# Key features by cyclic shifts in three products, dense queries spread through DRAM, and a third pair of banks, in a two-block attention kernel

## The chip, the cores and the metric

The kernel runs on one core of a Trainium2 chip. The metric is the device time of one execution in microseconds (us). Several executions are timed for each kernel, and one more is recorded by the profiler; its length is called the span, and is about 2 us shorter than the time (429.1 us for 431.45 in before). A run is called slow when it lies over 1.5% above the fastest of the same kernel; such runs are left out of every ratio.

Engines are named as the profile names them: PE (matmul), PEld (its weight loads), DVE (VectorE), ACT (ScalarE), POOL (GpSimd), SP (the queue that issues all DMAs here but two loads of 800 KB, which ACT issues). The sums of PE's matmuls land in the PSUM tile `ps`, which this kernel declares as eight banks of 512 fp32 numbers per partition, 0 to 7.

## The reference

Two attention blocks over different inputs, S = 2048, D = 640, 32 heads of 20, their outputs put side by side:

```python
def _A_ref(x, wqkv, wo):                       # softmax attention
    qkv = (x @ wqkv).reshape(B, S, 3, H, Dh).transpose(2, 0, 3, 1, 4)
    q, k, v = qkv[0], qkv[1], qkv[2]
    p = softmax(einsum("bhqd,bhkd->bhqk", q, k) * Dh ** -0.5)
    o = einsum("bhqk,bhkd->bhqd", p, v)
    return o.transpose(0, 2, 1, 3).reshape(B, S, D) @ wo

def _B_ref(x, wqkv, wo):                       # linear attention
    ...                                        # the same q, k, v
    phi = lambda t: where(t > 0, t + 1, exp(t)) + 1e-6
    pq, pk = phi(q), phi(k)
    num = einsum("bhqd,bhde->bhqe", pq, einsum("bhsd,bhse->bhde", pk, v))
    den = einsum("bhqd,bhd->bhq", pq, einsum("bhsd->bhd", pk))[..., None] + 1e-6
    return (num / den).transpose(0, 2, 1, 3).reshape(B, S, D) @ wo

output = concatenate([A, B], axis=-1)          # [1, 2048, 1280]
```

## The kernel before

Block A does not form the 2048 x 2048 scores. The scores are small, so the exponential is replaced by a polynomial of second order, and `exp(q.k)` becomes a scalar product of features: a constant, the 20 entries of k, and the 210 products of pairs of them. A guard on the chip checks that the scores are small and falls back to an exact path otherwise. So there are three stages:

1. For each of 16 tiles of 128 keys: project K and V, make the pair products on DVE and ACT (the tile `F`), and add `V^T F` into four banks on PE.
2. For each of 32 units (512 queries, 4 heads): a *select* matmul (`f_Qr`, `f_S`) puts sums of two query entries in banks, ACT squares them (four squares of 1024 columns per unit), a last group of matmuls multiplies the squares with the sums of stage 1, and DVE moves the result to `OTr`. After two units the *normaliser* follows: the denominators go out to DRAM, and come back as one 512 KB load `Rbc` that repeats them over partitions; a DVE multiply divides.
3. A rest, in which the last normalisers and the output projections run.

Block B has few dependences on A, and its matmuls fill gaps. The order of each engine's instructions is fixed when the kernel is built: a planner simulates the engines with durations written into the source, and takes the ready task with the lowest `prio` number. A wrong duration cannot give a wrong result, but it gives a poor order.

The parts (cuts marked with `...`):

```python
    NPS = 2          # buffers for the squares
    NP = 3           # buffers for pairs waiting for their normaliser
    NRB = 1          # buffers for the broadcast load

    def t_feat(self, t, deps):                 # 19 products a tile, of 64 to 640 elements
        ...
        sets = ((5, 10, 15), (1, 4, 9, 14, 19), (2, 7, 8, 13, 18), (3, 6, 11, 12, 16, 17))
        for ds in sets:
            def fn(_, ds=ds):
                for d in ds:
                    L = _DL[d]
                    o = self.F[:, s, :, _DO[d]:_DO[d] + L]
                    a = self.F[:, s, :, 220:220 + L]
                    b = self.Ks[:, s2, :, d - 1:d - 1 + L] if d % 2 else self.F[:, s, :, 220 + d:220 + d + L]
                    sch.op("dve", lambda e, o=o, a=a, b=b: e.tensor_tensor(o, a, b, op=ALU.mult), ...)
        ...

    def t_q(self, n, deps):                    # queries of one unit, weights padded from 20 to 32 columns
        ...
            for c in range(N_DC):
                self.fm(ps[:, b, :], self.wq[:, c, g, :], self.xT[:, qc, c, :], ...)

    def t_sel(self, n, k, deps):
        ...
            for i in range(4):
                sch.mm(ps[0:_NF, i, :], self.S2[...], self.Qr[32 * i:32 * i + 32, s, :], ...)   # banks 0 to 3
        j = self.plan.add(_Task("pe", 0.22, fn, prio=0.7, acq=("sA", "sB"), mode="sc"), deps)
        for p in range(2):                     # one square for banks 0, 1 and one for banks 2, 3
            ...

    def t_norm(self, P, evs):
        ...
        nb = nd.rearrange("(i u) q -> i (u q)", u=2).unsqueeze(1).broadcast_to([4, 32, 1024])
        d3 = self.spd([lambda e: e.dma_start(self.Rbc[:, rb].rearrange("p u q -> p (u q)"), nb)], (d2, prev), ...)

        def mult(_):
            sch.op("dve", lambda e: e.tensor_tensor(self.OTw[:, ow], self.OTr[:, pr], self.Rbc[:, rb], op=ALU.mult), ...)
        ...
```

## Time and profile before

| | before |
|---|---|
| time, median of the first 3 runs | 428.57 us (427.08 to 433.26) |
| busy: PE, DVE, ACT | 328.6, 304.1, 220.5 us of a span of 429.1 (the profiled run took 431.45 us) |
| span up to the first square | 177.7 us |
| first square to the end of the last | 198.0 us |
| after the last square | 53.4 us |

The three stretches are cut from the trace at the first and the last square of ACT. The busy tenths of the page, 40 slices of the span, show the stages: DVE full up to slice 16, PE full afterwards, a thin last eighth. PEclk is the clock that PE was granted, in tenths of full speed.

```profile
PE   3295677778777776899898778979998898765176
DVE  4849999999999999677678435546785686454631
ACT  1163457446354434587888676546766387600001
PEclk9998899999899989799999878789999898959589
```

The windows view gives busy times per stretch. Its columns are the stretch, its length, then the busy us and the number of instructions of PE, PEld, DVE, ACT and POOL, the granted clock, the DMA share and GB/s. The rows are the middle of stage 1, the squares, and the rest.

```profile
40.00:160.00 120.00, 91.40 (x2540) 64.43 (x2536) 112.04 (x320) 59.91 (x155) 0.00 (x0) 0.96 0.11 26
177.70:375.70 198.00, 173.31 (x2956) 81.47 (x2952) 128.29 (x251) 138.97 (x166) 0.00 (x0) 0.93 0.41 122
375.70:429.10 53.40, 30.18 (x541) 17.58 (x541) 22.44 (x47) 2.55 (x7) 0.00 (x0) 0.75 0.40 122
```

In stage 1 DVE is busy 112 of 120 us, and PE 91. In the squares PE is the fullest with 173 of 198. In the rest no engine is.

The costliest groups, from the page. After the bar stand busy us and the mean ns of one; after the second bar the idle time just before them and what ended it.

```profile
L1364 ACT ACTIVATE f_big<-ps 110x1024 bf16<-110x1024 f32 x128 | 123.8, 1026 | 50.5 <-PE ps L172 50.5
L1235 DVE TENSOR_TENSOR f_big<-f_big,f_Ks 128x512 bf16<-128x512 bf16 (+9 forms) x160 | 54.6, 345 | 4.4
L172 PE MATMUL ps<-f_xT,f_wq 128*32 128x512 bf16 x640 | 43.5, 413 | 1.0 <-DVE f_big L1393 1.0
L1235 DVE TENSOR_TENSOR f_big<-f_big 128x320 bf16<-128x320 bf16 (+3 forms) x144 | 47.6, 330 | 4.6
L1448 DVE TENSOR_TENSOR f_OTw<-f_big,f_Rbc 128x1024 bf16<-128x1024 f32 x15 | 18.3, 1221 | 20.7 <-DMA f_Rbc<-f_Nd 20.7
```

The two product groups are 102 us of DVE in 304 instructions. ACT waits 50.5 us for the selects. DVE waits 20.7 us for the broadcast load; DVE is not the bound of the squares.

The chain that ended last, by engine and by line:

```profile
PE 38%; DVE 37%; ACT 9%; DMA 8%; issue 3%; POOL 2%; SPq 1%; DVEq 0%; POOLq 0%; ACTq 0%
```

### The profile page before, as it was taken

The page shows a single profiled execution, that of the slowest core. Times are in us where ns is not written, and L with a number is a line of the kernel's source. Part 1 is how long each engine was busy: PE and PEld are TensorE (multiplying, and loading weights), DVE is VectorE, ACT ScalarE, POOL GpSimd, SP SyncE. Part 2 cuts the span into 40 slices and gives each one's busy share as a digit, 9 for nine tenths or more (in the row PEclk, how much of TensorE's full clock was granted, in tenths as well). Part 3 has the DMA queues.
Part 4 walks back from the last instruction along what each step waited for, and adds up shares of the span by engine and source line. Part 5 has one row for each costly group of instructions (what it writes and reads, how often), then busy time and mean ns, then how long its engine had stood idle before and what let it go on. Part 6 is the DMA issues. An engine that isn't in the chain of part 4 may idle for free.

```text
span 429.1 us, 14778 instructions
## 1 busy us (share of the span) xinstructions
PE 328.6 (77%) x6596; PEld 184.5 (43%) x6596; DVE 304.1 (71%) x734; ACT 220.5 (51%) x371; POOL 12.8 (3%) x52
## 2 busy tenths in 40 slices
PE   3295677778777776899898778979998898765176
PEld 0263454556455554565343222435344442443042
DVE  4849999999999999677678435546785686454631
ACT  1163457446354434587888676546766387600001
POOL 6400000000000000000000000000000000000000
PEclk9998899999899989799999878789999898959589
DMA  8969530000000000000413455733345644684131
GB/s 290 255 147 122 112 128 2 4 3 3 3 4 3 2 4 3 2 4 5 130 55 108 136 131 173 223 133 113 115 131 155 192 127 118 191 229 155 57 110 65
DMA packets 53124, 42.26 MB, mean 98 GB/s; under 512 B 22624, under 2 KB 48576, under 8 KB 53056
## 3 DMA queue, kind: packets, MB, share of 16 engines
q1 hardware_dynamic: 51744, 39.64, 33.3%
q10 hardware_dynamic: 1312, 1.64, 1.0%
q8 instruction: 52, 0.85, 0.8%
q14 instruction: 16, 0.13, 0.1%
HBM read 23.63 MB, written 13.19 MB: 86 GB/s over the span
## 4 chain that ended last, share of the span: by engine, by line
PE 38%; DVE 37%; ACT 9%; DMA 8%; issue 3%; POOL 2%; SPq 1%; DVEq 0%; POOLq 0%; ACTq 0%
PE ps L172 38%; DVE f_big L1235 23%; ACT f_big L1364 8%; DMA out_dram<-f_st 5%; DVE f_kn L1241 2%; DVE f_pk L1529 2%; DVE f_r L1521 2%; DMA f_Rbc<-f_Nd 2%; POOL f_it L1114 1%; SPq L1666 1%; DVE f_st L1026 1%; DVE f_CT L1138 1%; DMA f_w<-f_Od 1%; ACT f_ex L1525 1%; DVE f_big L1393 1%
## 5 line engine op out<-in xcount | busy, mean ns | idle before, releaser
L1364 ACT ACTIVATE f_big<-ps 110x1024 bf16<-110x1024 f32 x128 | 123.8, 1026 | 50.5 <-PE ps L172 50.5
L172 PE MATMUL ps<-f_w,f_xT 128*32 128x320 bf16 x1280 | 52.4, 319 | 13.3 <-ACT f_ex L1525 9.4
L1235 DVE TENSOR_TENSOR f_big<-f_big,f_Ks 128x512 bf16<-128x512 bf16 (+9 forms) x160 | 54.6, 345 | 4.4
L172 PE MATMUL ps<-f_wB,f_xB 128*32 128x320 bf16 x1280 | 51.6, 310 | 4.7 <-DVE f_woB L1599 2.5
L1235 DVE TENSOR_TENSOR f_big<-f_big 128x320 bf16<-128x320 bf16 (+3 forms) x144 | 47.6, 330 | 4.6
L1525 ACT ACTIVATE f_ex<-ps 128x320 f32<-128x320 f32 (+1 forms) x52 | 26.0, 500 | 44.0 <-DVE f_r L1521 43.8
L172 PEld LDWEIGHTS ps<-f_w,f_xT 128*32 128x32 bf16 x1280 | 35.2, 103 | 28.3 <-ACT f_ex L1525 12.2
L172 PE MATMUL ps<-f_Qr,f_S 32*110 32x512 bf16 x256 | 35.2, 437 | 15.0 <-ACT f_big L1364 15.0
L1026 DVE CAST f_st<-ps 128x320 bf16<-128x320 f32 x54 | 25.0, 484 | 30.2 <-PE ps L172 18.7
L172 PE MATMUL ps<-f_xT,f_wq 128*32 128x512 bf16 x640 | 43.5, 413 | 1.0 <-DVE f_big L1393 1.0
L172 PEld LDWEIGHTS ps<-f_wB,f_xB 128*32 128x32 bf16 x1280 | 33.5, 100 | 19.4 <-ACT f_big L1217 4.5
L1521 DVE TENSOR_SCALAR f_r<-ps 128x320 f32<-128x320 f32 (+1 forms) x52 | 29.3, 565 | 9.4 <-PE ps L172 9.1
L172 PE MATMUL ps<-f_woB,f_pk 128*32 128x320 bf16 x640 | 25.4, 311 | 13.5 <-DVE f_pk L1700 13.4
L1393 DVE TENSOR_SCALAR_CACHE_REDUCE f_big<-ps,f_c 128x512 f32<-128x512 f32 x32 | 23.9, 748 | 15.4 <-PE ps L172 15.2
L1448 DVE TENSOR_TENSOR f_OTw<-f_big,f_Rbc 128x1024 bf16<-128x1024 f32 x15 | 18.3, 1221 | 20.7 <-DMA f_Rbc<-f_Nd 20.7
L172 PE MATMUL ps<-f_big,f_Vp 128*32 128x241 bf16 x512 | 18.0, 288 | 18.8 <-DVE f_big L1235 18.8
L172 PE MATMUL ps<-f_wo,f_w 128*32 128x320 bf16 (+1 forms) x584 | 28.5, 339 | 4.1 <-DMA f_w<-f_Od 2.2
L1022 ACT CAST f_st<-ps 128x320 bf16<-128x320 f32 x10 | 4.2, 426 | 50.8 <-PE ps L172 32.2
L172 PE MATMUL ps<-f_big,f_Tu 110*32 110x512 bf16 x256 | 27.3, 436 | 2.6 <-ACT f_big L1364 2.5
L172 PEld LDWEIGHTS ps<-f_Qr,f_S 32*110 32x110 bf16 x256 | 10.5, 124 | 43.7 <-ACT f_big L1364 28.9
L1026 DVE CAST f_Qr<-ps 128x512 bf16<-128x512 f32 x28 | 19.3, 688 | 14.1 <-PE ps L172 14.1
L1022 ACT CAST f_big<-ps 128x320 bf16<-128x320 f32 x31 | 12.9, 427 | 31.1 <-PE ps L172 23.8
(113 smaller groups left out, 382.2 us busy)
## 6 DMA issues: line engine op xcount, KB each, us to landing
f_Rbc<-f_Nd SPq DMA_DIRECT2D x15, 512.0 KB
f_Bd<-f_dc SPq DMA_DIRECT2D x16, 320.0 KB, 6.5
f_w<-f_Bd SPq DMA_DIRECT2D x20, 256.0 KB, 8.5
out_dram<-f_st SPq DMA_DIRECT2D x32, 160.0 KB, 4.6
f_wB<-in_B_wqkv_dram SPq DMA_DIRECT2D x3, 800.0 KB, 5.4
f_Od<-f_OTw SPq DMA_DIRECT2D x60, 40.0 KB
f_w<-f_Od SPq DMA_DIRECT2D x3, 640.0 KB
f_w<-in_A_wqkv_dram ACTq DMA_DIRECT2D x2, 800.0 KB
```

The lines of the kernel that those rows point to most:

```text
L172: lambda e: e.matmul(out, lhsT, rhs, start=start, stop=stop, tile_position=tp, skip_group_check=sgc),
L1022: return self.sch.op("act", lambda e: e.copy(out, in_), reads=reads, writes=writes)
L1026: return self.sch.op("dve", lambda e: e.tensor_copy(out, in_), reads=reads, writes=writes)
L1114: sch.op("pool", lambda e, d=d, k=k: e.iota(it[:, 1 + k, _DO[d]:_DO[d] + _DL[d]], [[1, _DL[d]]], base=d * k, channel_multiplier=0), writes ...
L1235: sch.op("dve", lambda e, o=o, a=a, b=b: e.tensor_tensor(o, a, b, op=ALU.mult), reads=rd, writes=(("F", s, "q"),))
L1241: sch.op("dve", lambda e: e.tensor_reduce(self.kn[:, t, :], self.F[:, s, :, 0:20], axis=AX.X, op=ALU.add), reads=(("F", s, "d", 0), ("F", ...
L1364: sch.op("act", lambda e: e.activation(self.psi[0:_NF, sp, k, 2 * p:2 * p + 2, :], ps[0:_NF, 2 * p:2 * p + 2, :], AF.Square, scale=sc), re ...
L1393: sch.op("dve", lambda e: e.tensor_scalar(self.OTr[:, pr, u, :], ps[:, j.bank, :], self.cst[:, g:g + 1], 0.0, op0=ALU.add, op1=ALU.max, ac ...
L1448: sch.op("dve", lambda e: e.tensor_tensor(self.OTw[:, ow], self.OTr[:, pr], self.Rbc[:, rb], op=ALU.mult), reads=(("Rbc", rb, 0), ("Rbc", ...
L1521: sch.op("dve", lambda e: e.tensor_scalar(r1, ps[:, j.bank, 0:n], 0.0, 1e-6, op0=ALU.max, op1=ALU.add), reads=(("ps", j.bank),), writes=(( ...
L1525: sch.op("act", lambda e: e.activation(ex, ps[:, j.bank, 0:n], AF.Exp), reads=(("ps", j.bank),), writes=(("ex", k),))
L1529: sch.op("dve", lambda e: e.scalar_tensor_tensor(dst, ex, 1.0, r1, op0=ALU.min, op1=ALU.add), reads=(("ex", k), ("r1", k)), writes=(res,) ...
```

## The change

Its intent is to take DVE out of the bound in stage 1, fill the freed PE time there with work from later, and let PE and ACT overlap in the squares.

1. **Products.** The differences d = 1 to 19 become cyclic shifts. Nine full shifts and one half shift give the same 190 pairs, so one instruction makes all five odd shifts (3200 elements), one the four even (2560), one the half (320). The key operand is repeated with a zero step. ACT makes shifted copies and one square of 640 from SBUF.
2. **Queries.** The projection is dense (400 matmuls instead of 640), done in stage 1, stored to DRAM (`Qd`) and loaded spread out into `Qr`.
3. **Ring.** The selects rotate through three pairs of banks instead of two; all other work of the squares keeps banks 6 and 7. The selects also get a better priority.
4. **Buffers.** `NP` 3 to 5, `NRB` 1 to 2, `NPS` 2 to 3; `OTr` moves onto the dead tile `xT`.
5. **B's keys and values** move forward (priority number 3.0 to about 1.02).
6. **B's denominators** are stored once for each of the four blocks of 512 queries (32 rows) and repeated by 52 loads of whole heads in all, instead of four stores of repeated rows for each block and 20 plain loads in all.
7. **Planner.** Many durations and the order of the loads are changed; POOL clears `Qr` (8192 elements) instead of `wq` (5120), and makes 31 index rows instead of 40.

The diff, cut to its core:

```diff
-    NPS = 2
-    NP = 3
-    NRB = 1
+    NPS = 3
+    NP = 5
+    NRB = 2
...
-    def t_feat(self, t, deps):
+    def t_feat(self, t, kd, deps):
...
-        sets = ((5, 10, 15), (1, 4, 9, 14, 19), (2, 7, 8, 13, 18), (3, 6, 11, 12, 16, 17))
-        for ds in sets:
-            def fn(_, ds=ds):
-                for d in ds:
...
+        ke = bass.AP(k0.tensor, k0.offset + 2, [pa[0], pa[1], [2, 4], [1, 20]])
...
+        ko = bass.AP(s0.tensor, s0.offset, [pb[0], pb[1], [2, 5], [1, 20]])
+        def odd(_):
+            sch.op("dve", lambda e: e.tensor_tensor(
+                F[:, :, 112:212].rearrange("p h (d a) -> p h d a", a=20), k0.unsqueeze(2).broadcast_to([128, 32, 5, 20]),
+                ko, op=ALU.mult), ...)
...                                   # t_Tfin: who owns the banks in the squares
-            evs.append(self.any(1000, ev, (last,), prio=0.1, rel=((("sA", 0),) if hf == 0 else (("sB", 2),)), k=4))
+            evs.append(self.any(1000, ev, (last,), prio=0.1, k=4))
+        plan.add(_Task("none", 0.0, lambda t: None, rel=(("sel", 0), ("sel", 2))), evs)
+        plan.add(_Task("none", 0.0, lambda t: None, acq=("take45",), rel=(("sel", 4),)), evs)
...                                   # queries
-                self.fm(ps[:, b, :], self.wq[:, c, g, :], self.xT[:, qc, c, :], start=(c == 0), stop=(c == N_DC - 1),
+                self.fm(ps[:, b, :], self.w[:, 0, c, 128 * c2:128 * (c2 + 1)], self.xT[:, qc, c, :], start=(c == 0),
...
-        j = self.plan.add(_Task("pe", 0.22, fn, prio=0.7, acq=("sA", "sB"), mode="sc"), deps)
+        j = self.plan.add(_Task("pe", 0.22, fn, prio=0.4, acq=("sel2",), mode="sc"), deps)
...                                   # block B's denominators
-            m2 = self.spd([lambda e, j=j, bd=bd: e.dma_start(
-                bd[:, j], self.dc[j:128:4, :].unsqueeze(1).broadcast_to([32, D_HEAD, 128])) for j in range(4)],
-                (e2,), ("dc",), (("Bd", tc),))
+            m2 = self.spd([lambda e, bdw=bdw: e.dma_start(bdw, self.dc[:])], (e2,), ("dc",), (("Bd", tc),))
```

The broadcast load `Rbc` alternates between two buffers (one in `f_Rbc`, one in `f_big`).

## The prediction

> **What bounds the kernel now.** The windows show three stages.
>
> - 21-168 us, block A's key features. DVE is busy 17-19 of every 20 us, PE only 14-17. The lines view gives the products 54.6 + 47.6 = 102 us in 304 instructions, 6.4 us of a tile's 9.2 us. In the chain of waits, that product line alone is 23% of the span. DVE bounds this stage.
> - 178-380 us, queries. PE is busy 15-20 of every 20 us. ACT does 128 squares of 1026 ns (123.8 us busy) and waits 50.5 us for PE before them: the timeline shows a select matmul waiting for the square that empties its banks, then that square's successor waiting for the select. PE and the two-pair ring bound this stage (6.1 us a unit, 32 units).
> - 380-429 us, tail. PE is about half idle; 12 us of it is one wait behind the normaliser's broadcast load (DVE multiply idle 6.6 us on DMA).
>
> **What changes, costed from the trace.**
>
> 1. Products: 64 elements take 221 ns, 640 take 488: 0.46 ns an element plus 0.19 us. Three products of 3200, 2560 and 320 elements: 1.67 + 1.38 + 0.34 = 3.4 us (estimate), against 6.4 plus 0.5 of gaps. Saves about 3.4 us a tile, 55 us of DVE. [...]
> 2. ACT pays: shifted copies from SBUF (640 elements took 727 ns here) and one square, about 2.3 us a tile against 1.7. +9 us.
> 3. Query projection: 400 instead of 640 matmuls of 512 columns, 43.5 to about 27 us of PE; 20 evictions instead of 32, -8 us. It moves into stage 1 with the last quarter of B's keys and values (in stage 1 today: about 976 of 1280 matmuls). Stage 2 loses about 55 us of PE work; stage 1 gains about 35.
> 4. Three pairs let a select run while ACT squares. Price: two banks, not four, for everything else in stage 2. My estimate of bank-time there (32 outputs x 2.3, 20 B queries x 2.3, 20 numerators x 1.7, 64 projections x 1.7 us) is 260 us, over two banks 130 us: near-binding.
> 5. Deeper normaliser buffers and the smaller broadcast through DRAM (its four stores hold the SP queue 7.5 us a time) remove waits, mostly in the tail.
> 6. Start: nine fewer index instructions on POOL (-2 us), but a longer clear, and today the 110-element copy beside the clear takes 3.9 us; about even.
>
> **Critical path.** Stage 1 becomes PE-bound: per tile 2.9 + 2.9 (projections, at the 36 ns a matmul of dense stretches) + 1.0 (features) + 0.4 + 1.4 (queries) = 8.6 us, about 9.1 with today's clock: 146 us, the same length, doing 35 us more. Stage 2 then has PE about 130 us at lower clock, ACT about 145, DVE about 122, banks 130: I expect 160-175 us instead of 205. Tail 8-10 us shorter.
>
> Predicted: 380 us, 362 to 402. Faster by over 2%: 0.93; within: 0.05; slower: 0.02.
>
> **Right if:** products' busy time about 54 us in 48 instructions; DVE under 80% in stage 1 with PE over 85%; stage 1 ends near 170; ACT waits before squares fall from 50 below 25 us; PE busy about 310 us in all.
>
> **Wrong if:** [...] the two remaining banks starve PE in stage 2 (waits on evictions, 395 or more); [...] or the extra ACT copies delay the features.

About 170 us up to the first square, 160 to 175 for the squares and about 44 for the rest (53.4 less 8 to 10) come to about 380. The 3.4 us of the products rest on the 0.46 ns of the trace of before; that they would hold with a repeated operand was my estimate, which no trace had shown then. The "lower clock" of stage 2 is the 0.93 of the squares in before, against 0.96 from 40 to 160 us. The bank-times of 2.3 and 1.7 us are estimates too; in the trace of before, around 308 and 321 us, 20 matmuls of a query of B take 1.26 us and the two instructions that empty their bank 0.69 (DVE) and 0.60 (ACT); 20 of a projection take 0.86 and its one eviction 0.48.

## The result, and the profile after

The median of four runs is 396.47 us (393.0 to 398.3), against 428.84 us of before with its fourth run. The ratio is 0.922, with a 95% interval of 0.913 to 0.932. Here and below a ratio is the mean time of one kernel's fast runs over that of the fast runs of before of the same rounds, so it is not quite the ratio of the medians quoted. All twelve kernels of the experiments are on record as correct.

| us | before | after | foreseen for after |
|---|---|---|---|
| up to the first square | 177.7 | 174.2 | about 170 |
| first square to end of the last | 198.0 | 157.1 | 160 to 175 |
| after the last square | 53.4 | 63.3 | 8 to 10 shorter |
| span | 429.1 | 394.6 | time 380 |

So 41 us came out of the squares, 3.5 out of stage 1, and 10 were given back in the rest. The time lies inside the range, 16 us above its centre. The rest explains it: about 44 us were foreseen for it (53.4 less 9), 19 fewer than it took.

The same busy tenths after the change:

```profile
PE   4278997999999899598879787787896896357485
DVE  5859985876846988966625264575664877354431
ACT  1147864564757687448999975769785895010001
PEclk9999999999999999779966867989898999587789
```

Its windows, cut at its own first and last square:

```profile
40.00:160.00 120.00, 114.10 (x3344) 84.91 (x3344) 91.27 (x135) 80.44 (x180) 0.00 (x0) 1.00 0.25 66
174.20:331.30 157.10, 131.90 (x1727) 51.45 (x1723) 92.68 (x180) 129.59 (x147) 0.00 (x0) 0.87 0.38 114
331.30:394.60 63.30, 35.38 (x694) 20.83 (x686) 27.01 (x52) 2.94 (x8) 0.00 (x0) 0.81 0.39 129
```

In stage 1 PE and DVE changed places: 114 and 91 of 120 us, with 3344 matmuls where there were 2540. In the rest PE has 694 matmuls where it had 541, because B's output projection got less of its work done earlier (320 of its matmuls are left instead of 160). PE's busy time there grew from 30.2 to 35.4 us, and its idle time from 23.2 to 27.9.

The groups that answer to those of before:

```profile
L1457 ACT ACTIVATE f_big<-ps 100x1024 bf16<-100x1024 f32 (+1 forms) x128 | 120.8, 1043 | 16.5 <-PE ps L172 16.3
L1298 DVE TENSOR_TENSOR f_big<-f_big,f_Ks 128x3200 bf16<-128x3200 bf16 x16 | 28.9, 1820 | 1.8 <-ACT f_Ks L1065 1.8
L172 PE MATMUL ps<-f_xT,f_w 128*32 128x512 bf16 x400 | 23.8, 379 | 1.1 <-ACT f_Vp L1065 1.1
L1303 DVE TENSOR_TENSOR f_big<-f_big 128x2560 bf16<-128x2560 bf16 x16 | 23.7, 1484 | 0.0
```

With the half shift (5.5 us, 344 ns each) the products take 58.1 us in 48 instructions. The repeated operand, beside one whose rows overlap, nearly kept the rate of before: 640 more elements (3200 against 2560) cost 336 ns, 0.525 ns each. My own slope of 0.46 ns, taken from instructions of 64 to 640 elements, was too flat: from 320 to 640 alone the products of before, without a repeated operand, give 0.50 (328 and 488 ns).

ACT's wait for selects fell from 50.5 to 16.3 us. But DVE's waits for the broadcast load did not fall (lines of the view of waits: total us, times, longest). The first two lines are the two buffers of the load; the third is PE waiting for a multiply of block B.

```profile
DVE f_OTw L1543 <- DMA f_Rbc<-f_Nd: 12.1, 6, 4.5
DVE f_OTw L1543 <- DMA f_big<-f_Nd: 10.6, 3, 7.0
...
PE ps L172 <- DVE f_pk L1807: 7.3, 2, 6.1
```

They add up to 22.7 us, against 20.7 before. And DMA has become a quarter of the chain that ended last:

```profile
PE 43%; DMA 24%; DVE 17%; ACT 7%; issue 3%; SPq 3%; POOL 2%; DVEq 0%; POOLq 0%; ACTq 0%
PE ps L172 43%; DMA f_Rbc<-f_Nd 11%; DMA out_dram<-f_st 5%; DVE f_big L1298 4%; DMA f_big<-f_Nd 3%; ACT f_big L1457 3%; DMA f_w<-f_Od 3%; DVE f_r L1620 2%; DMA f_Nd<-f_Rc 2%; ACT f_ex L1624 2%; DVE f_big L1303 2%; DVE f_CT L1182 2%; SPq L15
```

The two destinations of the one load make 14% of the chain, about 57 us. The chain's longest piece outside PE is one such load, at the border of the squares and the rest. By the packet records its first packet came 5.9 us after the issue: the load before it was still moving. The lines give the start, the length and what it was:

```profile
327.70 12.94 DMA f_Rbc<-f_Nd
340.70 1.11 issue
341.81 0.69 DVE f_pk L1807
342.50 0.04 issue
342.55 4.49 PE ps L172 x64
```

The timeline of the same moment shows how a DMA that only DVE waits for stops PE. The brackets give the idle time before an instruction, and what ended it.

```profile
340.67 1.23 DVE L1543 TENSOR_TENSOR f_OTw<-f_xT,f_Rbc 128x1024 bf16<-128x1024 f32 x1 [4.48 <-DMA f_Rbc<-f_Nd]
...
341.81 0.68 DVE L1807 TENSOR_TENSOR f_pk<-ps,f_w 128x512 bf16<-128x512 f32 x1
...
342.55 7.20 PE L172 MATMUL ps<-f_woB,f_pk 128*32 128x320 bf16 x144 [6.12 <-DVE f_pk L1807]
```

DVE takes its instructions in a fixed order. The multiply for A's normaliser stands in front and waits 4.48 us for the load. B's multiply stands behind it and cannot pass, though PE had finished its operand at 335.9 us; PE waits 6.12 us for B's multiply.

### The profile page after: what moved, and what is told of

Read it like the earlier page. It is cut to its first block, busy times and chain, and to the rows that moved or that the text cites. A ratio compares the mean times of both kernels' runs of the same rounds, so it can differ in the third digit from the quotient of the medians.

```text
span 394.6 us, 14071 instructions
## 1 busy us (share of the span) xinstructions
PE 315.4 (80%) x6356; PEld 179.0 (45%) x6356; DVE 251.6 (64%) x444; ACT 232.9 (59%) x373; POOL 14.2 (4%) x43
## 4 chain that ended last, share of the span: by engine, by line
PE 43%; DMA 24%; DVE 17%; ACT 7%; issue 3%; SPq 3%; POOL 2%; DVEq 0%; POOLq 0%; ACTq 0%
PE ps L172 43%; DMA f_Rbc<-f_Nd 11%; DMA out_dram<-f_st 5%; DVE f_big L1298 4%; DMA f_big<-f_Nd 3%; ACT f_big L1457 3%; DMA f_w<-f_Od 3%; DVE f_r L1620 2%; DMA f_Nd<-f_Rc 2%; ACT f_ex L1624 2%; DVE f_big L1303 2%; DVE f_CT L1182 2%; SPq L1552 1%; DVE f_st L1069 1%; DVE f_OTw L1543 1%
## 5 line engine op out<-in xcount | busy, mean ns | idle before, releaser
L1457 ACT ACTIVATE f_big<-ps 100x1024 bf16<-100x1024 f32 (+1 forms) x128 | 120.8, 1043 | 16.5 <-PE ps L172 16.3
L172 PE MATMUL ps<-f_Qr,f_S 32*110 32x512 bf16 (+1 forms) x256 | 41.4, 472 | 7.5 <-ACT f_big L1457 7.4
L1488 DVE TENSOR_SCALAR_CACHE_REDUCE f_xT<-ps,f_c 128x512 f32<-128x512 f32 x32 | 23.6, 736 | 20.1 <-PE ps L172 19.9
L172 PEld LDWEIGHTS ps<-f_woB,f_pk 128*32 128x32 bf16 x640 | 18.6, 113 | 27.5 <-DVE f_pk L1807 8.5
L172 PE MATMUL ps<-f_xB,f_wB 128*32 128x512 bf16 x400 | 29.5, 426 | 1.9 <-ACT f_ex L1624 1.8
L1298 DVE TENSOR_TENSOR f_big<-f_big,f_Ks 128x3200 bf16<-128x3200 bf16 x16 | 28.9, 1820 | 1.8 <-ACT f_Ks L1065 1.8
L172 PE MATMUL ps<-f_big,f_Tu 110*32 110x512 bf16 (+1 forms) x256 | 26.2, 441 | 1.1 <-ACT f_big L1457 0.9
L172 PEld LDWEIGHTS ps<-f_wo,f_w 128*32 128x32 bf16 (+1 forms) x584 | 16.3, 103 | 22.3 <-DMA f_w<-f_Od 10.0
L172 PE MATMUL ps<-f_xT,f_w 128*32 128x512 bf16 x400 | 23.8, 379 | 1.1 <-ACT f_Vp L1065 1.1
L1303 DVE TENSOR_TENSOR f_big<-f_big 128x2560 bf16<-128x2560 bf16 x16 | 23.7, 1484 | 0.0
```

The costliest lines, as they stand in the source:

```text
L172: lambda e: e.matmul(out, lhsT, rhs, start=start, stop=stop, tile_position=tp, skip_group_check=sgc),
L1298: sch.op("dve", lambda e: e.tensor_tensor(F[:, :, 112:212].rearrange("p h (d a) -> p h d a", a=20), k0.unsqueeze(2).broadcast_to([128, 32, ...
L1303: sch.op("dve", lambda e: e.tensor_tensor(F[:, :, 22:102].rearrange("p h (d a) -> p h d a", a=20), k0.unsqueeze(2).broadcast_to([128, 32, ...
L1457: sch.op("act", lambda e: e.activation(self.psi[0:nb, sp, k, 2 * p:2 * p + 2, :], ps[0:nb, b:b + 2, :], AF.Square, scale=sc), reads=(("ps" ...
L1488: sch.op("dve", lambda e: e.tensor_scalar(self.OTr[:, pr, u, :], ps[:, j.bank, :], self.cst[:, g:g + 1], 0.0, op0=ALU.add, op1=ALU.max, ac ...
```

## The experiments

Twelve kernels were run in three groups of four. The kernels of a group share one chip and the runs of before on it (medians 429.97, 431.18 and 429.06 us). The kernel after was not run again beside them, so it is compared through the ratios to before. Names with `e_` start from the kernel after, `b_` from the kernel before. Where a ratio is given, the interval of 95% follows in brackets.

### e_prod19: the products cut again into 19, nothing else

```diff
+        def one(o, x, y, rd, w):
+            for k in range(2):
+                h = slice(10 * k, 10 * (k + 1))
+                sch.op("dve", lambda e, h=h: e.tensor_tensor(o[:, :, h], x[:, :, h], y[:, :, h], op=ALU.mult), ...)
...
-            sch.op("dve", lambda e: e.tensor_tensor(F[:, :, 112:212]..., k0.unsqueeze(2).broadcast_to([128, 32, 5, 20]), ko, ...))
+            for j in range(5):
+                one(F[:, :, 112 + 20 * j:132 + 20 * j], F[:, :, 212:232], Ks[:, :, 2 * j:2 * j + 20], ...)
```

(The even shifts likewise.) The layout, copies, order and all else stay those of after.

> The kernel after with its three products of a tile cut into 19 products of at most 320 elements (same values, same order of all engines' work, as the planner is not told). From the fit of the trace of before the products should cost about 6.5 us a tile instead of 3.65, so DVE gets about 46 us more, all in the first stage. Theory (the saving on DVE is what lets stage 1 carry the moved matmuls): DVE is busy 106 of stage 1's 140 us, 152 would not fit, stage 1 grows by 20 to 30 us and the run takes 415 to 426 us. Rival (stage 1 of the kernel after is set by PE and the saving is mostly slack): less than 6 us slower, at most 402 us.

It took 446.08 us, ratio 1.036 [1.029, 1.043]. DVE's busy time rose from 251.6 to 293.8 us, and the first square came at 222.6 us instead of 174.2. The squares (155.7) and the rest (65.9) stayed nearly as they were. So 42 us of DVE work cost 48 us, all in stage 1: the count of instructions matters at full price there. That is beyond both my theory (415 to 426 us) and its rival. But this kernel's planner still believed in three short products, so part of that price could be its order. The next run takes that away.

### e_prod19p: the same, with the planner told

```diff
-        a = self.dve(1.7, odd, [kd[0]] + deps, prio=1.6)
-        b = self.dve(1.75, even, [kd[1]] + deps, prio=1.6)
+        a = self.dve(3.4, odd, [kd[0]] + deps, prio=1.6)
+        b = self.dve(3.1, even, [kd[1]] + deps, prio=1.6)
```

> The 19 cut products again, and now the planner is told their cost (3.4 and 3.1 us for the two groups), so that it orders all engines' work for them: the change without its saving on the products. The run without telling was 446 us, 16 us slower than the kernel before. Theory (the products' saving carries the gain; without it the rest of the change is worth little or nothing): 420 to 445 us. Rival (the loss was an order made for short products, and a fitting order hides them): 398 to 412 us.

It took 429.71 us, ratio 0.999 [0.995, 1.003] (one of its four runs counts as slow). The first square came at 214.8 us, the squares took 156.7 and the rest 52.5. PE waits for the products, where after has 4.5 us of that:

```profile
PE ps L172 <- DVE f_big L1311: 27.0, 11, 6.1
```

Telling the planner gave back some 16 us of e_prod19's loss. The rest of the loss stays, and it is the whole gain of the change: everything in it but the three products, taken together and well planned, is worth nothing. The squares are 41 us shorter, and stage 1 is 37 us longer, since it took on the queries and B's keys and values without having DVE time for them. The products alone are not shown to be worth 33 us either: they pay because the freed time is used.

### e_q640: as many query matmuls as before

```diff
+            for c in range(3):
+                self.fm(ps[:, b, :], self.w[:, 0, c, 128 * c2:128 * (c2 + 1)], self.xT[:, qc, c, :], start=(c == 0),
+                        stop=(c == 2), reads=(("w", 0), ("xT", c, qc)), writes=(("ps", b),), inc=False)
```

Three of each five matmuls are done twice (the first sum is overwritten), which makes 640 again.

> The kernel after with 12 more matmuls of 512 columns ahead of each of the 20 query projections (640 in all as before; they are overwritten, result unchanged, order unchanged). About 16 us of PE work more, all in stage 1. Theory (stage 1 is now bound by PE): 10 to 17 us slower, 406 to 414 us, PE busy above 19 of 20 us in stage 1. Rival (stage 1 is bound by DVE, ACT or evictions and PE has room): less than 4 us slower.

It took 403.57 us, ratio 0.938 [0.932, 0.944]. PE's busy time grew by 11.4 us (315.4 to 326.8), the time by 7, the first square came 10 us later. That lies between my theory (10 to 17 us slower) and its rival (under 4). Stage 1 after the change therefore follows PE, though not one for one in the end. The 240 matmuls that the dense projection saves are worth about 7 us; its 12 saved evictions are not in this number.

### e_rings2: two pairs of banks for the selects, the third given back to the other work

```diff
-        plan.add(_Task("none", 0.0, lambda t: None, acq=("take45",), rel=(("sel", 4),)), evs)
```

> The kernel after with two rings of banks for the squares as before, banks 4 and 5 left to the other work. Theory (the third ring is what stops ACT waiting): the wait of ACT before the squares rises from 16 to 35-50 us, the stage of squares grows from 157 to 170-180 us, the run is 8 to 20 us slower. Rival (the third ring only moved the shortage to the other jobs, which have two banks instead of four): within 4 us of the kernel after, or faster, with less time lost in the tail.

It took 421.63 us, ratio 0.980 [0.973, 0.987]. The squares took 206.5 us and the rest 39.0; ACT's wait for selects was back:

```profile
ACT f_big L1456 <- PE ps L172: 54.3, 38, 5.6
```

So the third pair is worth some 25 us, most of the gain, and more than the 8 to 20 that I had expected. The squares are even longer than before's 198.0, although they hold less PE work (2086 matmuls for 2956). The selects' new priority (0.4) was chosen for three pairs and stayed here. The granted clock in the squares was 0.79, against 0.87 in after and 0.93 in before, and PE was busy 10 us more than in after over the span, for the same 6356 matmuls. Whether the priority or the clock is a reason is not separated.

### e_norm31: the old depths of the normaliser's buffers

```diff
-    NP = 5
-    NRB = 2
+    NP = 3
+    NRB = 1
```

> The kernel after with the normaliser's buffers of before (three result slots instead of five, one broadcast slot instead of two). Theory (the slow broadcast load sets the pace of the second stage, and more slots let it overlap): the load of the next pair must wait for the multiply of this one, ACT's wait before squares rises above 30 us, the run is 15 to 35 us slower, 411 to 431 us. Rival (the slots are not what it waits for): within 5 us of the kernel after.

It took 418.37 us, ratio 0.972 [0.967, 0.978]. The squares took 187.4 us, the rest 53.9. The waits:

```profile
ACT f_big L1457 <- PE ps L172: 42.5, 24, 6.3
DVE f_OTw L1543 <- DMA f_Rbc<-f_Nd: 37.2, 10, 9.0
```

So the deeper buffers are worth some 22 us, nearly as much as the ring. They do not shorten the load (first to last packet 6.74 us here, 6.45 in after): they let other work pass while it runs. All of that gain lies in the squares (187.4 us here, 157.1 in after); the rest is even shorter here than in after (53.9 and 63.3).

### e_rings2_norm31: both at once

The two edits above together.

> The kernel after with both the two rings and the normaliser's buffers of before (each alone cost 22 to 25 us): what is left of the change is the products, the dense queries and the moved matmuls. Theory (the ring and the buffers each serve a different wait of the second stage): losses add, 435 to 448 us, slower than the kernel before. Rival (with two rings the squares come slowly enough that the old buffers suffice): 420 to 428 us, as with two rings alone.

It took 422.2 us, ratio 0.984 [0.978, 0.989]: no slower than the ring's removal alone. The losses of 25 and 22 us do not add. The squares took 192.2 us and the rest 52.9, and DVE waited 48.5 us for the load. Ring and buffers complement each other: with either missing, the squares and the rest together take 241 to 246 us (245.5, 241.3 and 245.1 in the three runs), against 220.4 after and 251.4 before. So no single part can be called the cause of the gain; products, ring and buffers are each needed for most of it.

### e_rbc16: the broadcast load in four pieces

The load of 512 KB reads four rows, and repeats each over 32 partitions. Its source therefore starts with a dimension of 4. By the trace's packet records, 3.5 of its packets are in flight on the mean while the load moves, and it moves for 6.45 us. That this comes from the first dimension was my guess. The edit cuts it into one DMA for each of the four rows, whose source starts with the 32-fold repeat. The bytes and the packets of 4096 bytes stay the same. The edit changes the number of DMAs as well as the first dimension. The traces hold a control for that: block B's denominators are loaded in 2560 packets of 2048 bytes both in before, by 20 DMAs of 128 partitions, and in after, by 52 DMAs of whole heads, at most 6 in the first dimension. In before 6.6 of these packets are in flight on the mean, in after 3.4. So more DMAs did not put more packets in flight there. The first dimension fits both loads as the cause, but no run changes it alone.

```diff
-        d3 = self.spd([lambda e: e.dma_start(self.Rbc[rb].rearrange("p u q -> p (u q)"), nb)], (d2, prev),
-                      (("Nd", pr),), (("Rbc", rb, 0), ("Rbc", rb, 1)))
+        d3 = self.spd([lambda e, i=i: e.dma_start(self.Rbc[rb].rearrange("p u q -> p (u q)")[32 * i:32 * i + 32], nb[i])
+                       for i in range(4)], (d2, prev),
+                      (("Nd", pr),), (("Rbc", rb, 0), ("Rbc", rb, 1)), n=1)
```

(`n=1` leaves the planner's duration of the issue as it was, so the order of the instructions does not change.)

> The kernel after with each of the 15 broadcast loads of the normaliser (512 KB) issued as four loads of 32 partitions each whose source begins with the 32-fold repeat; order unchanged. In the trace of after the packets of such a load overlap only 3.6 deep[...]. Theory (the tail is long because the normaliser's chain of transfers is slow, and that load is its largest part, 9 to 13 us from issue): packets overlap 12 to 16 deep, the load lands in 4 to 6 us, the time after the last square falls from 63 to 48-55 us, the run is 8 to 15 us faster. Rival (the queue that issues is the limit, and three more issues of 0.55 us per load cost what the load gains): within 4 us, or slower.

It took 369.54 us, ratio 0.859 [0.851, 0.867], which is 27 us less than after. I had expected 8 to 15, and 12 to 16 packets in flight, a depth that no trace had shown for this load; there were 8.6. Its windows, at its own first and last square:

```profile
40.00:160.00 120.00, 114.48 (x3351) 85.61 (x3348) 92.89 (x138) 82.21 (x182) 0.00 (x0) 1.00 0.24 66
173.60:314.50 140.90, 126.45 (x1727) 48.86 (x1723) 92.79 (x179) 129.21 (x147) 0.00 (x0) 0.88 0.45 128
314.50:368.60 54.10, 34.80 (x694) 20.63 (x694) 26.49 (x52) 3.02 (x8) 0.00 (x0) 0.82 0.48 148
```

The matmul counts of the last two rows are those of after, 1727 and 694. The same work takes 140.9 us instead of 157.1, and 54.1 instead of 63.3. But 54.1 us is no shorter than the rest of before (53.4). The chain and the waits:

```profile
by line: PE ps L172 55.9%; ACT f_big L1457 6.1%; issue 3.8%; DVE f_big L1298 3.8%; DVE f_r L1621 3.5%; ACT f_ex L1625 3.0%; DVE f_big L1303 2.3%; DVE f_r L1175 2.2%; DMA f_Rbc<-f_Nd 1.4%; SPq L1787 1.3%; POOL f_Rbc L1159 1.3%; DVE f_pk L180
```

```profile
ACT f_big L1457 <- PE ps L172: 2.8, 6, 0.9
...
DVE f_OTw L1544 <- DMA f_Rbc<-f_Nd: 0.8, 1, 0.8
DVE f_OTw L1544 <- DMA f_big<-f_Nd: 0.7, 1, 0.7
```

DVE's waits for the load fell from 22.7 to 1.5 us, and ACT's for selects from 16.3 to 2.8. This run also settles a worry of the prediction: the two banks left to the other work are no bound, since the same two banks allow squares of 141 us. The load reached the squares by two paths: a `OTr` buffer comes free only after the multiply, and the multiply blocks DVE's queue as shown above. How much each path carried is not separated.

### b_rbc16: the same edit in the kernel before

> The kernel before with the normaliser's broadcast load split in four as in the run of the kernel after that took 369.5 us. Theory (the narrow load was there before too, but hidden behind PE and the two rings, and the change brought it to light): 3 to 12 us faster than the kernel before, 417 to 426 us. Rival (the narrow load costs both kernels the same): 20 to 30 us faster, 400 to 409 us.

It took 417.18 us, ratio 0.967 [0.964, 0.970]: a gain of 14 us, above the 3 to 12 of my theory and below the 20 to 30 of its rival. So the slow load was in the kernel before as well, and about half of it was hidden there behind other bounds. The squares went from 198.0 to 191.1 us, the rest from 53.4 to 47.0, and DVE's wait from 20.7 to 3.8 us. The same edit is worth twice as much after the change, when the squares run faster.

The 15 loads in the trace's packet records, means in us (the records have no engine numbers; packets in flight are the packets' time over the loads' movement):

```
kernel      issue to first packet   first to last   issue to last (longest)   packets in flight
before              1.69                6.68             8.37 (10.8)               3.8
after               3.26                6.45             9.71 (13.0)               3.5
e_norm31            1.80                6.74             8.54 (10.7)               3.7
e_bdold             2.78                6.58             9.36 (12.3)               3.6
e_rbc16             1.07                3.44             4.50 (6.4)                8.6
b_rbc16             1.15                2.90             4.06 (5.1)               10.3
```

The landing got 1.3 us later by the change (8.37 to 9.71), and all of that lies before the first packet. With one buffer (e_norm31) it is gone. In after three of the 15 loads were issued while the one before was still moving, as the second buffer allows, and their first packets came 5.6 to 6.9 us after the issue; in before and e_norm31 there was no such load. They make over half of the difference.

### e_bdold: block B's denominators as before

Undone: the single store of each block and the 52 loads of whole heads; back come four stores of repeated rows for each block, and the 20 plain loads.

```diff
-            m2 = self.spd([lambda e, bdw=bdw: e.dma_start(bdw, self.dc[:])], (e2,), ("dc",), (("Bd", tc),))
+            m2 = self.spd([lambda e, j=j, bd=bd: e.dma_start(
+                bd[:, j], self.dc[j:128:4, :].unsqueeze(1).broadcast_to([32, D_HEAD, 128])) for j in range(4)],
+                (e2,), ("dc",), (("Bd", tc),))
```

> The kernel after with block B's reciprocals spread as before: four stores that repeat every row 20 times, and one load of 128 partitions a chunk in place of two or three loads of whole heads. Theory (the loads of whole heads [...] hold it up): the normaliser's load lands sooner, 8 to 9 us instead of 9 to 13, the run is 4 to 12 us faster. Rival (the smaller traffic of the change helps, because the four stores hold the issuing queue 7.5 us a time): 3 to 10 us slower.

It took 391.25 us, ratio 0.910 [0.904, 0.916], some 5 us less than after; the two intervals overlap a little, so the gain is likely, not settled. My theory was that the many narrow loads collide with the broadcast load. It mostly fell: the load's landing went only from 9.71 to 9.36 us and its movement not at all (6.45 and 6.58). The squares took 157.1 us as in after, the rest 57.7 instead of 63.3. The DMA-issuing instructions of the SP queue after 150 us of the span sum to 122 us, against 135 in after and 101 in before. That is a candidate for the 5 us, not a shown cause. Either way, this part of the change, which I had counted as a gain, shows none.

### e_rbc16_bdold: both of the last two edits

> The kernel after with both mends: the normaliser's load split in four, and block B's reciprocals spread as in the kernel before. Alone they gave 27 us and about 5 us against the kernel after. Theory (both shorten the same chain of transfers, so little is left for the second once the first is in): 366 to 371 us. Rival (they act on different waits): 361 to 365 us.

It took 369.25 us, ratio 0.860 [0.856, 0.865]. That is the time of e_rbc16 alone. With the load mended, nothing is left of what the old denominators gained.

### e_rbc16_head: e_rbc16, and POOL's clear of `Qr` in 16 pieces

At the start, DVE copies 110 elements (`f_CT`) while POOL clears a large tile. The copy took 3.88 us in before beside a clear of 4.49, and 6.46 us in after beside 7.05. Both times the copy ended 0.05 us after the clear (at 14.75 and 14.70 us, and at 15.60 and 15.55). How a clear can hold the copy, no trace shows; that it does is what the edit tests. In e_rbc16 it was not the copy that stood still but an instruction in front of it, beside a clear of 6.92 us; it ended at 15.55 us, the clear at 15.42:

```profile
7.57 7.98 DVE L1175 TENSOR_SCALAR f_r<-f_Rbc,f_rp 128x210 f32<-128x210 int32 x1 [1.92 <-POOL f_Rbc L1159]
...
16.00 0.18 DVE L1182 COPY f_CT<-f_id 128x110 bf16<-128x110 bf16 x1
```

The edit:

```diff
-        sch.op("pool", lambda e: e.memset(self.Qr[:].rearrange("p k g q -> p (k g q)"), 0.0), writes=("Qz",))
+        qf = self.Qr[:].rearrange("p k g q -> p (k g q)")
+        for i in range(16):
+            sch.op("pool", lambda e, i=i: e.memset(qf[:, 512 * i:512 * (i + 1)], 0.0), writes=(("Qz0", i),))
+        sch.op("pool", lambda e: e.memset(qf[:, 0:2], 0.0), reads=tuple(("Qz0", i) for i in range(16)), writes=("Qz",))
```

> The kernel after with the split load, and with POOL's 7 us clear of the query tile cut into 16 clears of 512 elements. In the trace of the split-load run a DVE instruction took 7.98 us beside that clear, and PE's first transposes began at 16.9 us. Theory (DVE stands still for one whole POOL instruction): no DVE instruction of the start takes over 1.5 us, the transposes begin 4 to 6 us sooner, the run is 2 to 6 us faster, 364 to 368 us. Rival (what PE waits for at the start are the loads of x and of the weights): within 1.5 us.

The timeline of DVE in this run:

```profile
7.54 1.12 DVE L1175 TENSOR_SCALAR f_r<-f_Rbc,f_rp 128x210 f32<-128x210 int32 x1 [1.90 <-POOL f_Rbc L1159]
...
9.11 0.52 DVE L1182 COPY f_CT<-f_id 128x110 bf16<-128x110 bf16 x1
...
16.60 0.24 DVE L1204 TENSOR_SCALAR f_r<-f_Rbc 128x147 f32<-128x147 int32 x1 [5.27 <-POOL f_Rbc L1201]
```

The instruction that had stood still fell from 7.98 to 1.12 us, and the copy takes 0.52 us instead of the 6.46 in after. So the one long clear was the cause of their length. But the time is 370.24 us, ratio 0.864 [0.857, 0.870] (one of its runs counts as slow): nothing gained. A few instructions later DVE waits 5.27 us for an index row that POOL makes after the clear, so the clear still holds DVE up, only at another place. PE's transposes begin at 10.19 us instead of 16.92, but the first projection starts at 21.64 us, only 1.3 us earlier than in e_rbc16 (22.96), and the first square at 172.2 instead of 173.6. The stall was real, but taking it away moved the start by little and the time not measurably.

### e_all: e_rbc16 with the old denominators and the clear in pieces

> All three mends together: split load, block B's reciprocals spread as before, clear cut in 16. If each acts on its own wait: 357 to 364 us. If the second and third are absorbed: 366 to 371 us.

It took 368.99 us, ratio 0.859 [0.854, 0.864]. Four kernels now stand at 369 to 370 us within each other's intervals. The best version is thus e_rbc16 itself, the smallest edit of them: 14% under before, 7% under after. In its squares ACT is busy 129 of 141 us and PE 126, at a granted clock of 0.88 (0.50 and 0.67 in the windows from 200 to 220 and 220 to 240 us); these are what is left there.

## Why the prediction was right or wrong

- **DVE bounded stage 1, and the products would free it: right.** With 19 products and a well-told planner the whole gain is gone (ratio 0.999). In stage 1 DVE is now under 80% and PE over 85%, as foreseen (76% and 95% from 40 to 160 us).
- **The products at 54 us: right in mechanism, short in size.** 48 instructions took 58.1 us, where the 304 of before took 102. An element cost 0.525 ns instead of the 0.46 of the forecast: the slope was taken from short instructions.
- **ACT pays 9 us, queries about 27 us of PE: right and a little cautious.** ACT's work on features rose from 27.7 to 36.8 us; the dense projection took 23.8 us. PE in all was 315.4 us for a foreseen 310.
- **Stage 1 keeps its length: nearly right.** 174.2 us up to the first square for a foreseen 170. e_q640 shows that PE work there now costs time, about 0.6 us for each.
- **The squares at 160 to 175 us: slightly better than that,** 157.1; ACT's wait fell to 16.3 us (foreseen: below 25). The cause named, three pairs, is confirmed by e_rings2, with an addition that the prediction lacked: without the deeper buffers, or without the ring, most of the gain is lost (e_norm31, e_rings2, e_rings2_norm31).
- **"The two remaining banks": the worry was needless.** e_rbc16 runs its squares in 141 us on the same two banks.
- **PE "at lower clock" in the squares: right,** 0.87, against 0.93 in before, and against 1.00 from 40 to 160 us in after, where PE was busy 114 of 120 us. Over the span it was 0.905, against 0.913 in before.
- **The step that failed is point 5,** "Deeper normaliser buffers and the smaller broadcast through DRAM … remove waits, mostly in the tail", and its term in the sum, "Tail 8-10 us shorter". The rest grew by 10 us, from 53.4 to 63.3. Half of the growth is PE's busy time, with more work left over, half is idle time. The deeper buffers did remove waits, but what they gained lies in the squares: with the old ones (e_norm31) DVE waited 37.2 us for the load instead of 22.7 and ACT 42.5 us before squares instead of 16.3, the squares took 30 us more than in after, and the rest 9 us less. In the rest, PE's wait for B's multiply did shrink (13.4 to 7.3 us), but its wait for A's last results from DRAM (`f_w<-f_Od`) grew from 2.2 to 8.6. Over the span, DVE's waits for the broadcast load went from 20.7 to 22.7 us and DMA's share of the chain from 8% to 24%: the load landed no sooner (8.37 us, then 9.71). Mending the load itself took 9 us from the rest and 16 from the squares. That is about half of what the term was wrong by: the rest still took 54.1 us there, where about 44 were foreseen, with 320 matmuls of B's output projection left for it instead of 160, and a wait of 7.9 us for A's last results. How these two share the other half stays open. I had read "12 us … behind the normaliser's broadcast load" in the profile of before and trusted the buffers with it, without asking why that load took 8 us.
- **"The smaller broadcast" of block B was a mis-sized term too:** undoing it is likely a gain of 5 us (e_bdold).
- **The start was "about even": right,** the first K projection came 0.9 us later (22.19 instead of 21.34 us).

What stays open: what the planner's changed durations and load order, the third square buffer and B's earlier keys and values are worth by themselves; why e_rings2 has longer squares than before; and the cause of e_bdold's 5 us.

## What to carry to other kernels

When a change speeds up one stage, ask of each DMA that the stage waits for how long it takes and how many of its packets are in flight, and only then whether more buffers will hide it: here one load, a single DMA whose first dimension was 4, with 3.8 packets in flight before the change and 3.5 after it, cost 14 us and 27, against the same load as four DMAs with 10.3 and 8.6. In a queue with a fixed order, a wait of an engine that is not the bound becomes a wait of the one that is, as soon as the bound's next input stands behind it (in after, DVE waited 4.48 us for the load, and PE 6.12 us for the multiply behind that wait). And gains of a ring, of buffers and of shorter instructions need not add: take each one out of the finished kernel, with the planner told, before you give it a value.
